# Moving work between engines in a two-branch kernel: damping buffers, attention first, transposing loads, reciprocals on ScalarE

One Trainium2 chip, one core. The metric is device time in microseconds (us); lower is better. A single core has no neighbour to compare it with, so "fast" and "slow" below only mean: within or over 1.5% of the fastest run of the same kernel in the same call.

## The reference, cut to what matters

Two branches over 2048 positions and 448 channels, side by side in the output.

```python
# A: linear attention, 16 heads of 28, features are softmax(+p) and softmax(-p)
q, k, v = split(x @ wqkv)
phi_k = concat(softmax(k @ w_phi), softmax(-(k @ w_phi)));  phi_q likewise
o = (phi_q @ (phi_k.T @ v)) / (phi_q @ sum(phi_k) + 1e-6)
a = o @ wo
# B: a long convolution by FFT; its kernel comes from 256 states per channel
K = einsum(C, exp(dt * A * l), dt * B).real        # l = 0..2047
y = irfft(rfft(u) * rfft(K)) + u * Dskip
return concat([a, y], -1)                           # bf16
```

## The kernel before

Every operation is recorded with its engine and issued in a fixed, searched order (a list of operation numbers); a second list gives the PSUM banks, a third the operations that go to an alternative engine. So an engine that waits is never overtaken by later work of its own. Branch B goes through the channels in four quarters: `rotations` (sines), `hi_tables`, `dampings` (exponentials), `tables` (products, VectorE), `scatter_k`, then spectra and convolution. The parts that the argument touches:

```python
xT = sb(oX, [112, 4, 2048])                      # x transposed: contraction in 4 chunks of 112 rows
Wp = [sb(o, [112, 4, 448]) for o in (155392, 158976)]   # query and key weights, w_phi folded in
WV = sb(162560, [112, 4, 448])

def recip(o, a):                                  # twelve of these: 8 key pairs, 4 query tiles
    prog.add("V", lambda: low(lambda: nc.vector.reciprocal(o, a)))

def key_side():
    for pr in range(8):                           # 8 pairs of 128-position tiles
        EK = sb(177920 + 3584 * (pr % 2), ...)    # two buffers
        ET = sb(209216, [128, 14, 128])           # one buffer
        for t in range(2):
            mms(acc(psum[:, b4, 0:448], [(xT[:, dj, ts_], Wp[1][:, dj, :]) for dj in range(4)]))
            mms(acc(psum[:, b5, 0:448], [(xT[:, dj, ts_], WV[:, dj, :]) for dj in range(4)]))
            ...                                   # exponentials to EK, values to V
        # EK -> ET by a transposing DMA on the SyncE queue
        ...                                       # ET @ HZ: sums per head, into PSUM
        recip(rk, psum[:, bz, 0:64])
        mul(VR, V, rk)                            # VectorE
        ...                                       # EK.T @ VR added up in PSUM
```

x and the query and key weights were transposed by TensorE (`flip_x`, `fold_weights`). [cut: tables, spectra, convolution]

The softmax here doesn't subtract the row's maximum and nothing guards it: scores larger than these inputs give would overflow.

## Time and profile before

| | before |
|---|---|
| median of 3 runs | 288.65 us (286.94 to 290.14) |
| span of the profiled run | 284.6 us |
| busy: PE, DVE, ACT | 236.7, 255.6, 202.2 us |
| table loads of ScalarE | 11 |
| matmul instructions | 3932 |

The prediction below shows the stages and groups. Three more views of the kernel before are needed later. First the page's chain of work that ended last (shares of the span by engine), and its row of the granted TensorE clock in 40 slices:

```profile
DVE 36%; PE 32%; DMA 15%; issue 7%; ACT 5%; SPq 3%; POOL 1%; DVEq 0%; POOLq 0%
```

```profile
PEclk9999999999999999999779999998999959999999
```

Then what weight loads (PEld) waited for (sum, times, longest), and the groups of matmuls with 448 and 512 columns (busy, mean ns):

```profile
PEld L203 <- issue: 28.3, 68, 1.9
```

### The profile page before, as it was taken

What the parts mean: (1) busy time and instruction counts of PE and PEld (TensorE: products, weight loads), DVE (VectorE), ACT (ScalarE), POOL (GpSimd) and SP (SyncE); (2) the same over time, 40 slices, a digit from 0 to 9 for tenths busy, and PEclk for the clock granted to TensorE, in tenths of its full rate; (3) what the DMA queues carried; (4) which work ended last, traced back from release to release, by engine and by line L of the source; (5) the groups of instructions that cost most, each with busy time, mean ns of one, the idle gap of its engine ahead of it and who ended that gap; (6) DMA issues with size and microseconds to landing.
All of it is one profiled execution on the core that took longest, in us unless ns stands there. A gap on an engine that the chain in (4) does not pass through costs nothing.

```text
span 284.6 us, 8940 instructions
## 1 busy us (share of the span) xinstructions
PE 236.7 (83%) x3932; PEld 179.9 (63%) x3932; DVE 255.6 (90%) x285; ACT 202.2 (71%) x340; POOL 16.1 (6%) x32
## 2 busy tenths in 40 slices
PE   1149899999999999999288977896989789897884
PEld 1149565756556587746187435782577789896874
DVE  4497999999999999799999999997999999499990
ACT  3759998989769989997899886869376224524241
POOL 8012101200000000000000010000000100000000
PEclk9999999999999999999779999998999959999999
DMA  7999375675353432513062648187789384747043
GB/s 166 229 232 243 89 209 120 142 191 129 67 131 65 67 131 59 83 36 87 6 137 46 134 118 323 19 191 222 281 267 324 72 275 85 192 59 155 2 99 68
DMA packets 64071, 39.49 MB, mean 139 GB/s; under 512 B 46736, under 2 KB 59424, under 8 KB 63648
## 3 DMA queue, kind: packets, MB, share of 16 engines
q1 hardware_dynamic: 61024, 31.57, 46.6%
q0 software_dynamic: 3008, 7.34, 8.2%
q8 instruction: 31, 0.51, 0.8%
q14 instruction: 8, 0.07, 0.1%
HBM read 26.36 MB, written 8.85 MB: 124 GB/s over the span
## 4 chain that ended last, share of the span: by engine, by line
DVE 36%; PE 32%; DMA 15%; issue 7%; ACT 5%; SPq 3%; POOL 1%; DVEq 0%; POOLq 0%
DVE sbuf L164 33%; PE psum L203 31%; DMA sbuf<-SCd 7%; DMA sbuf<-in_A_x_dram 5%; ACT sbuf L192 3%; SPq L218 3%; ACT sbuf L195 2%; DMA SCd<-sbuf 1%; DVE sbuf L189 1%; DVE sbuf L176 1%; DMA out_dram<-sbuf 1%; DMA sbuf<-in_B_u_dram 1%; PE psum L213 1%; POOL sbuf L218 1%; ACT L192 0%
## 5 line engine op out<-in xcount | busy, mean ns | idle before, releaser
L203 PE MATMUL psum<-sbuf 128*16 128x48 bf16 (+10 forms) x3824 | 229.0, 256 | 36.0 <-DVE sbuf L164 10.5
L203 PEld LDWEIGHTS <-sbuf 128*16 128x16 bf16 (+4 forms) x3824 | 171.5, 109 | 91.1 <-issue 28.3
L164 DVE TENSOR_TENSOR sbuf<-sbuf 128x896 bf16<-128x896 bf16 (+13 forms) x220 | 217.2, 1033 | 10.4 <-PE psum L203 3.5
L195 ACT CAST sbuf<-psum 128x448 bf16<-128x448 f32 (+4 forms) x128 | 70.9, 605 | 55.7 <-PE psum L203 54.1
L192 ACT ACTIVATE sbuf<-psum 128x448 bf16<-128x448 f32 (+4 forms) x140 | 83.9, 668 | 9.9 <-PE psum L203 9.7
L192 ACT ACTIVATE sbuf<-psum,sbuf 128x896 bf16<-128x896 f32 (+3 forms) x28 | 21.9, 814 | 4.4 <-DVE sbuf L164 2.3
L195 DVE CAST sbuf<-psum 128x896 bf16<-128x896 f32 (+2 forms) x13 | 12.4, 974 | 7.7 <-ACT sbuf L192 5.7
L213 PE MATMUL psum<-sbuf 128*112 128x128 bf16 (+2 forms) x108 | 10.3, 259 | 8.2 <-DVE sbuf L164 7.0
L213 PEld LDWEIGHTS <-sbuf 128*112 128x112 bf16 (+2 forms) x108 | 9.1, 165 | 9.8 <-DMA sbuf<-in_A_x_dram 5.5
L192 ACT ACTIVATE sbuf<-sbuf 128x896 bf16<-128x896 bf16 (+3 forms) x13 | 11.8, 905 | 4.6 <-DVE sbuf L164 3.9
L192 ACT ACT_TABLE_LOAD x11 | 14.1, 1283 | 0.9 <-PEq L909 0.7
L218 POOL DMA_DIRECT2D sbuf<-const x4 | 2.2, 551 | 118.3 <-PE psum L203 118.1
L218 POOL DMA_DIRECT2D sbuf<-in_B_u_dram x8 | 6.5, 827 | 18.1 <-PE psum L213 17.8
L176 DVE TENSOR_SCALAR sbuf<-sbuf 128x896 bf16<-128x896 bf16 (+3 forms) x8 | 4.9, 609 | 1.7 <-ACT sbuf L192 1.5
L182 ACT COPY sbuf<-psum 128x128 f32<-128x128 f32 (+2 forms) x10 | 4.3, 427 | 2.6 <-PE psum L213 2.1
L218 POOL DMA_DIRECT2D sbuf<-SUd x4 | 2.1, 528 | 69.3 <-DVE sbuf L164 42.3
L164 DVE TENSOR_TENSOR sbuf<-psum,sbuf 128x128 f32<-128x128 f32 (+3 forms) x10 | 4.7, 492 | 0.5 <-ACT sbuf L182 0.4
L176 ACT ACTIVATE sbuf<-sbuf 128x448 bf16<-128x448 bf16 (+1 forms) x3 | 4.4, 1455 | 0.9 <-DVE sbuf L164 0.9
L189 DVE RECIPROCAL sbuf<-psum 128x64 bf16<-128x64 f32 x8 | 4.4, 550 | 0.1
L182 DVE COPY sbuf<-psum 112x1024 bf16<-112x1024 bf16 x6 | 4.1, 684 | 0.3 <-PE psum L213 0.2
L179 DVE SCALAR_TENSOR_TENSOR sbuf<-sbuf 128x64 f32<-128x64 f32 (+1 forms) x6 | 3.0, 505 | 0.0
L198 POOL MEMSET sbuf<- 128x32 bf16 (+3 forms) x6 | 1.4, 258 | 18.4 <-DVE sbuf L164 18.1
(17 smaller groups left out, 18.4 us busy)
## 6 DMA issues: line engine op xcount, KB each, us to landing
sbuf<-const SPq DMA_DIRECT2D x16, 384.0 KB, 4.9
SUd<-sbuf SPq DMA_DIRECT2D x8, 448.0 KB, 3.7
sbuf<-SCd SPq DMA_DIRECT2D x16, 224.0 KB
sbuf<-SUd POOLq DMA_DIRECT2D x4, 896.0 KB, 5.6
sbuf<-const POOLq DMA_DIRECT2D x2, 1024.0 KB, 7.4
sbuf<-in_A_x_dram SPq DMA_DIRECT2D x4, 448.0 KB, 15.0
out_dram<-sbuf SPq DMA_DIRECT2D x4, 448.0 KB, 3.2
sbuf<-in_B_u_dram SPq DMA_DIRECT2D x16, 112.0 KB, 3.1
```

The source lines that it names most:

```text
L164: prog.add("V", lambda: nc.vector.tensor_tensor(out=o, in0=a, in1=b, op=op))
L176: prog.add("V", lambda: nc.vector.tensor_scalar_mul(o, a, s), lambda: nc.scalar.activation(o, a, ACT.Copy, scale=s))
L179: prog.add("V", lambda: nc.vector.scalar_tensor_tensor(out=o, in0=a, scalar=s, in1=b, op0=op0, op1=op1))
L182: prog.add("V", lambda: nc.vector.tensor_copy(o, a), lambda: nc.scalar.copy(o, a))
L189: prog.add("V", lambda: low(lambda: nc.vector.reciprocal(o, a)))
L192: prog.add("A", lambda: nc.scalar.activation(o, a, fn, **kw))
L195: prog.add("A", lambda: nc.scalar.copy(o, a), lambda: nc.vector.tensor_copy(o, a))
L198: prog.add("G", lambda: nc.gpsimd.memset(o, v))
L203: nc.tensor.matmul(o, lhsT=l, rhs=r, **kw)
L213: nc.tensor.transpose(o, i, idn)
L218: prog.add(eng, lambda: e.dma_start(out=o, in_=i))
```

## The change

The intent: give the damping factors of the last quarter a buffer of their own, finish attention before the convolution starts (so that ScalarE, idle late, takes copies there), make VectorE's convolution products fewer and larger, and take work off TensorE and VectorE: half of x, the query weights and u's rows are transposed by DMA, u times Dskip becomes a matmul, and seven of twelve reciprocals become exp(-ln) on ScalarE. The diff, cut to its core:

```diff
-    def recip(o, a):
-        prog.add("V", lambda: low(lambda: nc.vector.reciprocal(o, a)))
+    def recip(o, a, t):
+        def by_exp():
+            nc.scalar.activation(t, a, ACT.Ln)
+            nc.scalar.activation(o, t, ACT.Exp, scale=-1.0)
+        prog.kind[len(prog.ops)] = "L"
+        prog.add("V", lambda: low(lambda: nc.vector.reciprocal(o, a)), by_exp)
+    # run(order, warm): warm() ahead of each run of exponentials that holds such a reciprocal
+    warm = lambda: nc.scalar.activation(sb(138112, [128, 1], F32), bias_hp, ACT.Ln)

-    xT = sb(oX, [112, 4, 2048]);  Wp, WV = [112, 4, D_MODEL]
+    xT = sb(oX, [128, 4, 2048]);  Wp, WV = [128, 4, D_MODEL]
+    def chunk(t, dj, *at):                        # 448 = 128 + 128 + 128 + 64
+        v = t[64:128, 3] if dj == 3 else t[:, dj]
+        return v[(slice(None),) + at]
-    mms(acc(..., [(xT[:, dj, ts_], Wp[1][:, dj, :]) for dj in range(4)]))
+    mms(acc(..., [(chunk(xT, dj, ts_), chunk(Wp[1], dj)) for dj in range(4)]))   # V, Q likewise

+    def flip(o, i):
+        prog.add("S", lambda: nc.sync.dma_start(out=o, in_=i, transpose=True))
+    def load_x_flipped(t):                        # second half of x: eight of these
+        flip(xq[:, 0:3, t, 256:512], x2[1024 + t::4, 0:384])
+        flip(xq[:, 3, t, 256:512], x2[1024 + t::4, 320:448])
+    def load_folded(which):                       # query weights: four
+        flip(wT[:, which, c, :], A_wqkv[:, c0:c0 + 128])

-        return sb((oW, 174336, 174336, oW)[qt], [128, 31, QC])       # damping factors
+        return sb((oW, 174336, 174336, oPW)[qt], [128, 31, QC])
-    dampings(3); tables(3); conv_loads(1, *CT); conv(1, *CT, (6, 7))
+    dampings(3); scatter_k(2); conv_loads(1, *CT); conv(1, *CT, (6, 7)); tables(3)
     # [cut: query_side(0..3) all before tables(1); products over both spectra at once;
     #  u * Dskip as a matmul with a diagonal; new order, banks and alternative engines]
```

The 128-row chunks come with the transposing loads: they are written in blocks of 128 channels, so the last chunk holds channels 320 to 447, of which rows 64 to 127 are new.

## The prediction

> **What bounds the kernel now.** I read the page first, then the busy time of each engine by stage, then the groups kept apart by shape, then the timeline where a stage ends. The page's totals and its rows of 40 slices:
>
> ```profile
> PE 236.7 (83%) x3932; PEld 179.9 (63%) x3932; DVE 255.6 (90%) x285; ACT 202.2 (71%) x340; POOL 16.1 (6%) x32
> ...
> DVE  4497999999999999799999999997999999499990
> ACT  3759998989769989997899886869376224524241
> ```
>
> DVE is full from slice 3 to the end. ACT is nearly as full until slice 28 (200 us) and then half empty. So ACT's 71% is an average of two stages. I cut the span where DVE begins the damping products of each quarter of the model's channels (57.7, 121.3, 157.3, 198.1 us):
>
> ```profile
> core 0: us, PE busy (x) PEld busy (x) DVE busy (x) ACT busy (x) POOL busy (x), PEclk, DMA share, GB/s
> 0.00:57.70 57.70, 40.58 (x406) 29.66 (x407) 47.30 (x55) 45.29 (x62) 12.89 (x26) 1.00 0.78 181
> 57.70:121.30 63.60, 61.80 (x923) 41.41 (x922) 60.12 (x69) 56.07 (x93) 0.00 (x0) 1.00 0.44 98
> 121.30:157.30 36.00, 28.33 (x606) 20.87 (x605) 35.38 (x43) 32.68 (x57) 0.00 (x0) 0.91 0.30 68
> 157.30:198.10 40.80, 32.62 (x597) 22.34 (x596) 38.46 (x41) 32.56 (x51) 1.59 (x3) 0.98 0.60 168
> 198.10:284.60 86.50, 73.37 (x1410) 65.58 (x1408) 74.36 (x82) 35.63 (x82) 1.57 (x3) 0.95 0.58 156
> ```
>
> In the columns after the length: PE, PEld, DVE, ACT, POOL busy. Stages 1 to 4 are DVE's (and PE's in the second), with ACT at 80 to 91%. Stage 5 (convolution) belongs to DVE and PE together; ACT has 51 us to spare there. The groups by shape that I use (busy, mean ns):
>
> ```profile
> L164 DVE TENSOR_TENSOR sbuf<-sbuf 128x3584 bf16<-128x3584 bf16 x35 | 70.2, 2021 | 0.8 <-ACT sbuf L195 0.3
> L164 DVE TENSOR_TENSOR sbuf<-sbuf 128x896 bf16<-128x896 bf16 x66 | 38.9, 622 | 1.0
> L164 DVE TENSOR_TENSOR sbuf<-sbuf 128x1792 bf16<-128x1792 bf16 x36 | 38.3, 1090 | 4.0 <-PE psum L203 3.5
> L189 DVE RECIPROCAL sbuf<-psum 128x64 bf16<-128x64 f32 x8 | 4.4, 550 | 0.1
> ```
>
> ```profile
> L192 ACT ACT_TABLE_LOAD x11 | 14.1, 1283 | 0.9 <-PEq L909 0.7
> ```
>
> The place that the first part of the change aims at is the head of stage 5, in the timeline of ACT and then of DVE:
>
> ```profile
> 192.51 1.28 ACT L192 ACT_TABLE_LOAD   x1
> 193.81 6.59 ACT L192 ACTIVATE sbuf<-psum 128x224 bf16<-128x224 f32 x11
> ```
>
> ```profile
> 198.12 0.63 DVE L176 TENSOR_SCALAR sbuf<-sbuf 128x1792 bf16<-128x1792 bf16 x1 [1.54 <-ACT sbuf L192]
> ...
> 200.43 1.91 DVE L164 TENSOR_TENSOR sbuf<-sbuf 128x3360 bf16<-128x3360 bf16 x1 [0.39 <-ACT sbuf L192]
> ```
>
> The last damping factors are made late, since they lie in the buffer of the rotated tables; DVE waits for them twice, 1.9 us in all. That is all that this wait costs.
>
> **What the Trainium skill says.** (1) "ScalarE: Activation LUTs", What ACT_TABLE_LOAD costs: about 1283 ns, plus a drain of about 1380 ns. The trace agrees on the first, 1283 ns in 11 loads; the drain isn't seen as extra time (a copy ends at 192.50, the load starts at 192.51, the next activation at 193.81). (2) The same page, Table sets: natural logarithm and exponential share one set, so one after the other should need one load. The kernel before has no logarithm, so no trace here shows it; the built program of the changed kernel contradicts it, see below. (3) "DMA: Bandwidth & Descriptors", DMA Transpose (X-bar): transposes run in the DMA, from the SP or ACT queue, for two-byte types. The trace has eight, of 128 x 1792 elements, which land in 4.0 us after some 1.5 us of the SP queue; I take that size for the new ones.
>
> **The change, part by part**, from the built order of both kernels.
>
> *DVE.* The convolution's products become larger, fewer instructions: 9 of 3584 columns go (-18.2 us), 3 of 7168 come (+11.7, scaled from 3.65 us for 6720), 3 more of 2x1792 (+6.1), 8 more of 1792 in sum (+8.7; twelve come, and the four of u times Dskip go, which PE now does with a diagonal matrix), 24 of 896 go (-14.9). That is -6.6 us, nearly all in stage 5. Seven of twelve reciprocals move to ACT: -3.9. The rest comes to about nil. DVE: 255.6 to 245.
>
> *PE.* 112 matmuls fewer: half of x, the query weights and a second set of arguments for the angles go (about -12 us of 236.7). The 816 matmuls of 128x112 (43.7 us) in stage 5 stay.
>
> *ACT.* Each moved reciprocal is a logarithm and an exponential of 64 columns. The kernel puts a dummy logarithm ahead of such stretches, plainly so that a set holding both functions stays loaded. In the built program this fails: every logarithm loads a set without the exponential, and the next exponential loads the old set again. It has **26 table loads in place of 11**: +15 x 1.283 = +19.2 us. The small activations themselves are 16 x 0.25 = +4. Rates 3, 11 and 13 in place of a second group of four: +7. Query exponentials over two banks: 32 x 0.606 to 16 x 1.06 = -2.4. Wider or moved copies: -10. Sum about +17: ACT 202 to 219, and since stage 5 loses 7, stages 1 to 4 gain 23.
>
> Now by stage. I add every ACT and DVE instruction of the new order between the same marks at its mean duration from the groups, less 0.074 us each for ACT (my sum for before is 227.5 against 202.2 busy over 340: neighbours overlap).
>
> - Stage 1: ACT 55.6 (was 45.3, five loads more) and some 9 idle at the start as now: 63 (now 57.7).
> - Stage 2: ACT 66 (was 56.1, four moved reciprocals of two loads each), DVE 53; with 2 us for the chain exponential, transpose, sum, reciprocal, product, which now has 3.1 us of reciprocal where it had 0.55: 68 (now 63.6). ACT has taken DVE's place.
> - Stage 3: ACT 40.5 (five loads more than it needs), DVE 39: 42 (now 36.0).
> - Stage 4: DVE 33.5, ACT 28: 35 (now 40.8). The own buffer pays here: damping factors no longer wait for PE to have read the tables, and attention is done.
> - Stage 5: DVE 70 after its start (was 74.4), then the last two inverse transforms and the store, 7 us as now (277.2 to 284.6), and 2.5 of waits, of which there are 5 now: 79.5 (now 86.5).
>
> Sum 63 + 68 + 42 + 35 + 79.5 = 287.5 against 284.6. Untraced runs take 288.65 - 284.6 = 4.05 more than the span: **291.5 us**. In words: about 13 us are gained late, on DVE, and 16 are lost early, on ACT.
>
> **The rivals.** (A) *The loads hide.* ACT had 21.8 us idle between 20 and 200 us, so 19 could fit. Then DVE keeps the bound: 284.6 - 10.5 of DVE work - some 5 of waits = 269, or 273 us. For it: DVE's order is fixed and it hardly waited for ACT so far. Against it: stage 3 has ACT at 91% already, and ACT's order is fixed too, so a load stands in front of whatever comes next; a product waits behind its reciprocal. It would also go this way if the program that runs had fewer loads than the one built here. (B) *The loads cost in full.* If ACT also stalls for its inputs in stages 1 to 3 as it does now (some 15 us there), while it carries 23 more, stage 5 starts near 218 rather than 208, and the time is about 301. For it: one buffer for the transposed exponentials ties ACT's next pair to DVE's product. Against it: an engine that is late finds its inputs ready. (C) *The new transposes stall the SP queue*: sixteen more, at 1.5 us of queue and 4 us to landing. In the early stage DMA is at 0.78 already and stores of the signal's spectrum stand behind them. But x's second half is needed only by the fifth pair of key tiles, and u's rows only in stage 5, at 0.58; I give this 0 to 3 us. (D) *PE becomes stage 5's bound*: 43.7 us of inverse transforms and spectra all after the last tables. DVE has 48 us beside them, so about equal; a granted clock below 1 there (0.95 now) would cost 2 to 3 us.
>
> **Range and chances.** The centre lies between A (273) and B (301), nearer B, since the loads are counted and not guessed. 8 in 10: 279 to 301. Faster by over 2% means under 282.9, which needs A at least by half: 0.2. Slower by over 2% means over 294.4, a step of 3 us from the centre: 0.33. Within: 0.47.
>
> **What would show it.** Right: 26 table loads of 1.28 us; ACT busy 215 to 222 and DVE 243 to 248; ACT at 95% or more from 60 to 170 us, DVE with waits for ACT of several us in stages 2 and 3 where it has almost none now; the first product of the last quarter at 203 to 213 us; some 79 us from there to the end; no wait for damping factors there. Wrong: 11 to 14 loads; DVE above 95% from 60 to 200 us; the last quarter's products before 195 us; a wait for a transposed tile of over 3 us; PE waiting for rows of u; the tail of stage 5 longer than 84 us.

## More of the kernel before

```profile
L203 PE MATMUL psum<-sbuf 112*128 112x448 bf16 x256 | 54.6, 360 | 2.4 <-DVE sbuf L164 2.1 <-ACT sbuf L195 0.3
...
L203 PE MATMUL psum<-sbuf 112*112 112x512 bf16 x64 | 16.1, 381 | 0.8 <-ACT sbuf L195 0.7
```

Read "112*128 112x448": 112 rows of contraction, 128 columns of weights, 448 columns streamed. The chain is VectorE's first, TensorE's second; weight loads wait 28 us in all, in 68 places, for nothing that the profile names.

The kernel before scatters by up to 2.6% within a call (282.63 to 289.88 us).

## The result, and the profile after

The changed kernel is **slower**: 309.62 us median (308.96 to 311.04, four runs, all fast) against 287.79 (286.36 to 290.14). Ratios here are the mean time of one kernel's fast runs over that of the other's in the same rounds, so not quite the ratio of these medians: 1.0756, 95% interval 1.0668 to 1.0845. That is outside the predicted range.

The changed kernel's page: totals, rows of 40 slices, and the chain that ended last.

```profile
PE 244.9 (80%) x3820; PEld 167.7 (55%) x3820; DVE 248.4 (81%) x256; ACT 217.9 (71%) x350; POOL 16.3 (5%) x32
...
PEclk9999799977989997997999667796998999999999
...
PE 42%; DVE 23%; DMA 13%; ACT 10%; issue 8%; SPq 3%; DVEq 0%; ACTq 0%
```

TensorE has 112 matmuls fewer and is busy 8 us **longer**. The chain has gone from VectorE to TensorE, and the clock row has many more slices of 6 to 8 than before. Busy time by stage, cut at the same marks as in the prediction (columns: length, PE, PEld, DVE, ACT, POOL, clock, DMA share, GB/s):

```profile
0.00:72.94 72.94, 48.09 (x398) 25.90 (x398) 51.93 (x61) 53.52 (x84) 13.02 (x26) 0.93 1.04 156
72.94:145.68 72.74, 64.44 (x887) 38.02 (x887) 55.83 (x63) 59.80 (x97) 0.00 (x0) 0.93 0.31 75
145.68:191.48 45.80, 37.97 (x626) 23.25 (x625) 38.20 (x43) 42.60 (x69) 1.12 (x2) 0.85 0.41 118
191.48:228.12 36.64, 28.28 (x488) 17.86 (x488) 35.22 (x32) 28.65 (x48) 0.53 (x1) 0.86 0.63 146
228.12:306.80 78.68, 66.17 (x1424) 62.64 (x1423) 67.18 (x61) 33.38 (x56) 1.58 (x3) 0.98 0.63 155
```

| stage | before | predicted | after |
|---|---|---|---|
| 1 | 57.7 | 63 | 72.9 |
| 2 | 63.6 | 68 | 72.7 |
| 3 | 36.0 | 42 | 45.8 |
| 4 | 40.8 | 35 | 36.6 |
| 5 | 86.5 | 79.5 | 78.7 |

The late stages are as predicted: 12 us won. Stages 1 to 3 miss by 10, 5 and 4 us. What VectorE waited for longest in the changed kernel (L204 is the exponential of a moved reciprocal, L206 a reciprocal left on VectorE, L222 a matmul):

```profile
DVE sbuf L177 <- ACT sbuf L204: 10.6, 4, 4.0
DVE sbuf L206 <- PE psum L222: 7.2, 2, 4.3
```

Its groups of table loads, 26 in all, by the line that needed them:

```profile
L211 ACT ACT_TABLE_LOAD x10 | 12.8, 1283 | 0.9 <-PEq L998 0.7
...
L203 ACT ACT_TABLE_LOAD x7 | 9.0, 1283 | 0.1
L204 ACT ACT_TABLE_LOAD x7 | 9.0, 1283 | 0.1
```

Its weight loads and matmuls with 64 rows, and the wait of weight loads for nothing that is named ("issue"):

```profile
L222 PEld LDWEIGHTS <-sbuf 64*128 64x128 bf16 x32 | 3.0, 94 | 14.1 <-issue 14.1
L222 PEld LDWEIGHTS <-sbuf 64*112 64x112 bf16 x16 | 2.0, 128 | 6.6 <-issue 6.6
```

```profile
L222 PE MATMUL psum<-sbuf 128*128 128x448 bf16 x224 | 54.3, 381 | 5.1 <-ACT sbuf L214 2.6 <-DMA sbuf<-const 1.1 <-DVE sbuf L214 0.8
...
L222 PE MATMUL psum<-sbuf 64*112 64x512 bf16 x16 | 7.2, 451 | 0.0
```

```profile
PEld L222 <- issue: 77.4, 184, 2.7
```

The timeline of weight loads, in one stretch of the key side, shows where these gaps lie:

```profile
78.65 0.30 PEld L222 LDWEIGHTS <-sbuf 128*128 128x128 bf16 x3 [0.20 <-issue]
79.32 0.09 PEld L222 LDWEIGHTS <-sbuf 64*128 64x128 bf16 x1 [0.37 <-issue]
79.62 1.54 PEld L222 LDWEIGHTS <-sbuf 112*128 112x128 bf16 x27 [0.20 <-issue]
81.53 0.09 PEld L222 LDWEIGHTS <-sbuf 64*128 64x128 bf16 x1 [0.37 <-issue]
```

Within these runs of 128- or 112-row loads no gap is listed. There is one of 0.37 us before each 64-row load and one of 0.20 us after it: with 48 such loads an estimate of 0.57 x 48 = 27 us over the kernel. The Trainium skill, "TensorEngine Tiling (Array Packing)", Key Properties, has a sentence that may fit: "Changing tiling mode (not just tile) drains the TensorE". No run here shows that 64 rows count as another mode; what the traces show is that a change between 112 and 128 rows, with 112 or 128 columns of weights and nothing named to wait for, leaves mostly 0 to 0.09 us, and that each of the 48 changes to 64 rows leaves the gap.

A third suspect stands in the chain of the changed kernel, in order of time (start, us, what):

```profile
55.59 12.26 DMA sbuf<-sbuf
67.85 0.05 issue
67.89 12.15 PE psum L222 x85
```

The third transpose of key features took 12.3 us to land; the prediction's size was 4.0, which the profile gives for one transpose of eight. TensorE waited for it, and the clock fell around it:

```profile
60.00:70.00 10.00, 5.69 (x47) 2.40 (x46) 5.38 (x6) 7.24 (x16) 0.00 (x0) 0.78 1.23 120
70.00:80.00 10.00, 10.00 (x71) 4.35 (x71) 6.96 (x14) 4.79 (x7) 0.00 (x0) 0.88 0.48 90
```

The skill's "TensorE: Matmul & The Clock Gate", Part 1, says that an idle window of about 3.4 us throttles the array; TensorE's longest wait in 20 to 75 us was 4.3 us, and in the kernel before the clock was 1.00 up to 121 us. That fits, but a long wait is not all that lowers the clock here. In the changed kernel it also fell where TensorE was busy throughout and had waited 2.1 us at most since 86 us:

```profile
116.80:120.20 3.40, 3.40 (x16) 1.63 (x15) 3.40 (x7) 2.36 (x3) 0.00 (x0) 0.50 0.02 5
```

What brings that about is not shown. The mean granted clock was 0.92 in the changed kernel against 0.97 in the kernel before, and no run separates that from the causes below.

So three theories, which do not exclude each other. **T1**: the reciprocals on ScalarE and their 15 extra table loads. **T2**: the transposing loads of x and query weights. **T3**: the 64-row chunk. T1 and T2 were in the prediction as rivals B and C. T3 was in no part of it.

### The profile page after: what moved, and what is told of

Its sections match the earlier page's. It is cut to its first block, busy times and chain, and to the rows that moved or that the text cites. A ratio compares the mean times of both kernels' runs of the same rounds, so it can differ in the third digit from the quotient of the medians.

```text
span 306.8 us, 8682 instructions
## 1 busy us (share of the span) xinstructions
PE 244.9 (80%) x3820; PEld 167.7 (55%) x3820; DVE 248.4 (81%) x256; ACT 217.9 (71%) x350; POOL 16.3 (5%) x32
## 4 chain that ended last, share of the span: by engine, by line
PE 42%; DVE 23%; DMA 13%; ACT 10%; issue 8%; SPq 3%; DVEq 0%; ACTq 0%
PE psum L222 42%; DVE sbuf L177 22%; DMA sbuf<-const 5%; DMA sbuf<-sbuf 4%; DMA sbuf<-in_B_B_re_dram 4%; ACT sbuf L211 3%; ACT sbuf L214 3%; ACT L203 2%; SPq L236 2%; SPq L240 1%; ACT sbuf L189 1%; ACT L204 0%; ACT sbuf L204 0%; PE psum L232 0%; ACT sbuf L203 0%
## 5 line engine op out<-in xcount | busy, mean ns | idle before, releaser
L222 PE MATMUL psum<-sbuf 128*16 128x48 bf16 (+9 forms) x3760 | 240.5, 260 | 52.7 <-DVE sbuf L177 11.6
L177 DVE TENSOR_TENSOR sbuf<-sbuf 128x1792 bf16<-128x1792 bf16 (+15 forms) x203 | 213.3, 1091 | 34.6 <-ACT sbuf L204 10.6
L222 PEld LDWEIGHTS <-sbuf 128*16 128x16 bf16 (+3 forms) x3760 | 163.5, 110 | 128.1 <-issue 77.4
L214 ACT CAST sbuf<-psum 128x448 bf16<-128x448 f32 (+3 forms) x93 | 66.0, 754 | 56.2 <-PE psum L222 51.7
L211 ACT ACTIVATE sbuf<-psum,sbuf 128x224 bf16<-128x224 f32 (+3 forms) x36 | 22.7, 701 | 0.0
L211 ACT ACT_TABLE_LOAD x10 | 12.8, 1283 | 0.9 <-PEq L998 0.7
L232 PE MATMUL psum<-sbuf 128*128 128x128 bf16 (+1 forms) x60 | 5.9, 245 | 5.4 <-DVE sbuf L177 3.4
L203 ACT ACT_TABLE_LOAD x7 | 9.0, 1283 | 0.1
L204 ACT ACT_TABLE_LOAD x7 | 9.0, 1283 | 0.1
L232 PEld LDWEIGHTS <-sbuf 128*128 128x128 bf16 (+1 forms) x60 | 4.7, 125 | 7.0 <-DVE sbuf L177 3.6
L206 DVE RECIPROCAL sbuf<-psum 128x64 bf16<-128x64 f32 x3 | 1.7, 555 | 7.2 <-PE psum L222 7.2
L189 DVE TENSOR_SCALAR sbuf<-sbuf 128x3584 bf16<-128x3584 bf16 (+3 forms) x7 | 5.0, 707 | 0.1
L189 ACT ACTIVATE sbuf<-sbuf 112x448 bf16<-112x448 bf16 (+3 forms) x4 | 3.8, 944 | 0.1
L177 DVE TENSOR_TENSOR sbuf<-psum,sbuf 128x896 bf16<-128x896 f32 (+2 forms) x6 | 3.5, 625 | 0.0
```

Source lines behind the costliest of these rows:

```text
L177: prog.add("V", lambda: nc.vector.tensor_tensor(out=o, in0=a, in1=b, op=op))
L189: prog.add("V", lambda: nc.vector.tensor_scalar_mul(o, a, s), lambda: nc.scalar.activation(o, a, ACT.Copy, scale=s))
L203: nc.scalar.activation(t, a, ACT.Ln)
L204: nc.scalar.activation(o, t, ACT.Exp, scale=-1.0)
L211: prog.add("A", lambda: nc.scalar.activation(o, a, fn, **kw))
L214: prog.add("A", lambda: nc.scalar.copy(o, a), lambda: nc.vector.tensor_copy(o, a))
```

## The experiments

Fourteen kernels. Medians are of all runs; "before" is the kernel before in the same call.

| label | median | before | fast ratio to before (95%) |
|---|---|---|---|
| (the changed kernel) | 309.62 | 287.79 | 1.0756 (1.0668 to 1.0845) |
| e1_one_set | 299.95 | 287.26 | 1.0607 (1.0473 to 1.0741) |
| e2_recip_dve | 300.89 | 287.26 | too few fast runs |
| e3_plain_x (wrong) | 299.38 | 287.26 | 1.0554 (1.0389 to 1.0718) |
| e4_rows128 | 296.72 | 287.26 | 1.0505 (1.0424 to 1.0585) |
| e5_set_rows | 285.70 | 287.27 | too few fast runs |
| e6_set_rows_plain (wrong) | 283.71 | 287.27 | 0.9937 (0.9834 to 1.0040) |
| e7_set_rows_pe (wrong) | 288.94 | 287.27 | 1.0048 (0.9935 to 1.0162) |
| e8_pairs (one run) | 305.70 | 287.27 | none |
| e9_order | 287.86 | 288.58 | 0.9992 (0.9926 to 1.0058) |
| e10_dve_rows | 286.89 | 288.58 | 0.9929 (0.9868 to 0.9990) |
| e11_pe_again | 294.85 | 288.58 | 1.0139 (1.0070 to 1.0209) |
| e12_two_moved | 304.98 | 284.73 | 1.0634 (1.0503 to 1.0765) |
| e13_wo_early | 303.70 | 287.41 | 1.0610 (1.0514 to 1.0706) |
| e14_repaired_wo_early | 285.53 | 287.41 | too few fast runs |

In the call of e1 to e4 only three of eight runs of the kernel before counted as fast (282.6 to 284.9), so its ratios lie higher than its medians say. Below, "won" is the drop of the median's distance from the kernel before, against the changed kernel's 21.8 us. It mixes fast and slow runs. By the fast ratios alone the wins are smaller: e1 4.3, e3 5.8, e4 7.2, e12 3.5, e13 4.2 us. So each size below is rough, to some 3 to 5 us.

### e1 and e2: the table loads

```diff
-    lambda: nc.scalar.activation(sb(138112, [128, 1], F32), bias_hp, ACT.Ln)       # e1
+    lambda: nc.scalar.preload_act_table_set("natural_log_exp_and_others")
-    (other if i in OTHER else fn)()                                                # e2
+    (other if i in OTHER and self.kind.get(i) != "L" else fn)()      # and no warm()
```

> The dummy logarithm ahead of each run of exponentials is replaced by an explicit load of the one table set that holds both functions; the built program then has 10 table loads in place of 26, so 16 x 1.283 us = 20.5 us less of ScalarE work. Theory T1 (the loads stand on the path: VectorE waited 10.6 us for ScalarE's exponential in the reciprocal and 7.2 us for PE behind it): 297 to 302 us, and those waits fall below 4 us. Rivals T2 (transposing loads of x hold up the early stages) and T3 (64-row contraction chunk slows TensorE): 306 to 310 us, because ScalarE is busy only 71% of the span and most loads fall into its gaps.

> All twelve reciprocals go back to VectorE, no logarithms at all; 10 table loads. T1: 296 to 302 us, at or a little below the one-set version, since a VectorE reciprocal took about 0.55 us against 3.1 us from logarithm to exponential. T2, T3: 306 to 310 us. If it is slower than the one-set version, the author's reciprocals on ScalarE are right once the loads are gone.

Both built to 10 table loads and both won 8 to 9 us (21.8 to 12.7, and to 13.6). In the one-set kernel VectorE's wait for the exponential is nearly gone:

```profile
DVE sbuf L177 <- ACT sbuf L204: 0.6, 1, 0.6
```

T1 holds, for some 9 of the 22 us. Its other sign failed: the wait for TensorE behind the reciprocal (L206) did not fall below 4 us, it was 10.1, so that wait was not the loads' (e13 below takes it to 1.1). Sixteen loads, 20.5 us of ScalarE, were worth 9 us of time, nearly all in stage 2 (72.7 to 64.6 us). The second finding is that reciprocals by ScalarE with the right set and by VectorE differ by less than the scatter.

### e3: the transposing loads

```diff
-    prog.add("S", lambda: nc.sync.dma_start(out=o, in_=i, transpose=True))     # x, query weights
+    prog.add("S", lambda: nc.sync.dma_start(out=o, in_=plain_rows_of_the_same_size))
```

> Wrong result on purpose: the twelve transposing loads of half of x and of the query weights become plain loads of about the same bytes into the same places at the same points of the order; the transposing loads of u and of the key features stay. T2: the first two stages shorten by 8 to 13 us together, total 297 to 302 us, the key-feature transposes land in about 4 us as before and the DMA share in 20 to 70 us falls below 1. T1, T3: 307 to 310 us.

It won 9.7 us. Taken alone that confirms T2. The DMA share in 20 to 30 us fell from 1.59 at 89 GB/s to 0.81 at 185 GB/s, so the plain loads do load the DMA engines far less (the share adds up packet times, so it can pass 1). The skill's "Advanced Engine Details and Errata", X-Bar Transpose (TRN2), says that transposing DMAs are as fast as regular ones; the profile gives the landing of one of the eight of x, 11.7 us (6.9 in e13, 14.7 in e2), and of one of the plain loads in their place, 6.4 (6.9 in e6), queueing included. So the trace speaks against it, on few landings. And the clock did not fall:

```profile
60.00:70.00 10.00, 9.83 (x75) 4.43 (x74) 9.05 (x15) 8.32 (x19) 0.00 (x0) 1.00 0.59 140
70.00:80.00 10.00, 9.65 (x88) 4.82 (x86) 8.91 (x4) 8.43 (x12) 0.00 (x0) 1.00 0.52 119
```

### e4 and e8: the 64-row chunk

```diff
-    v = t[64:128, 3] if dj == 3 else t[:, dj]                    # e4
+    v = t[:, dj]            # rows 0:64 of Wp[0][:, 3], Wp[1][:, 3], WV[:, 3] are set to zero
-    ... for dj in range(4)])])                                   # e8, query side only
+    ... for dj in (range(4), range(3, -1, -1))[k]])])
```

> The last contraction chunk of x and the weights is taken over all 128 rows, with rows 0 to 63 of the three weight blocks set to zero (two more small ScalarE copies, three POOL memsets), so the result stays right and each matmul has the same columns. T3 (a change between 64-row and 128-row tiles empties the array: weight loads of 64 rows idle 14.1 us and 6.6 us, PE 42% of the chain against 32%): PE idle of 15 to 20 us goes, of which 5 to 9 us on the path: 300 to 305 us; the mean of the 448-column matmuls falls from 390 to about 355 ns. T1, T2: 308 to 311 us.

> The changed kernel with the chunk order of every second query product turned round, so that the two 64-row matmuls of a pair stand side by side: as many 64-row matmuls, half as many changes between 64 and 128 rows on the query side. If the change of rows is what costs, the 6.6 us of idle before the sixteen 64-row weight loads of the query side fall to 3 to 4 us and the 64x512 matmul's mean falls from 451 ns; if a 64-row matmul is slow by itself, both stay. The time changes by less than 3 us either way: 306 to 310 us.

e4 does strictly more arithmetic than the changed kernel, and won 12.3 us, more than expected. PE is busy 232.6 us instead of 244.9, and the weight loads' unnamed wait fell by 19 us, as expected (15 to 20):

```profile
PEld L222 <- issue: 58.0, 103, 4.7
```

```profile
L222 PE MATMUL psum<-sbuf 128*128 128x448 bf16 x256 | 55.7, 369 | 5.2 <-ACT sbuf L214 2.8 <-ACT sbuf L203 1.3 <-DVE sbuf L214 0.7
```

The 32 matmuls with 64 rows and 448 columns had cost 12.7 us; as 32 more with 128 rows they add 1.4 to that group. The mean of that group fell from 381 to 369 ns only, not to the 355 expected. Two other things changed with the rows, so that the 12.3 us are not all theirs: the granted clock of the profiled run rose from 0.92 to 0.95, and TensorE's wait of 4.3 us for the key transpose is gone (see e13, which makes that worth up to 5.5 us). e8 says what it is about the 64 rows. It has as many 64-row matmuls, but on the query side two stand side by side, so TensorE goes over to 64 rows half as often there:

```profile
L222 PEld LDWEIGHTS <-sbuf 64*128 64x128 bf16 x32 | 3.0, 94 | 14.0 <-issue 14.0
L222 PEld LDWEIGHTS <-sbuf 64*112 64x112 bf16 x16 | 1.5, 132 | 3.5 <-issue 3.5
```

```profile
121.67 0.17 PEld L222 LDWEIGHTS <-sbuf 64*112 64x112 bf16 x2 [0.39 <-issue]
```

The query side's wait halved (6.6 to 3.5), the key side's, left as it was, stayed at 14; before the second load of a pair there is no gap, and the mean of the 64x512 matmul fell from 451 to 430 ns. So the gaps come with the going over, not with the 64 rows: T3 holds for its cause, while its size in time lies between some 7 and 12 us by medians. The time of e8 is one run, 3.4 us won, and the sum of all unnamed waits hardly moved (76.9 us), as other groups waited more; it only says that the sign is right.

### e5, e6, e10: together

e5 joins e1 and e4, e6 joins e1, e3 and e4, e10 joins e2 and e4.

> One table set for the reciprocals and the 128-row chunk together. Alone they took 9.7 and 12.9 us off 309.6. If the two costs are separate waits that stand on the path one after the other (T1 and T3 both true, independent): 286 to 289 us. If they cover each other (the same waits of VectorE seen twice): 293 to 297 us.

> As e5_set_rows, and with the transposing loads of half of x and of the query weights as plain loads (wrong result on purpose). Three independent costs: 309.6 - 9.7 - 12.9 - 10.2 = 276.8, so 275 to 280 us, faster than the kernel before, with the first three stages near the lengths predicted (63, 68, 42). If they overlap: 283 to 290 us.

> As e5_set_rows, with the reciprocals all on VectorE instead of on ScalarE with one table set. In the changed kernel the two repairs were worth the same (299.95 and 300.9 us), so 284 to 288 us here. If VectorE has become the engine that sets stage 2 (55.3 us busy of 56.1 in e5_set_rows), the added 3 us of it show in full: 287 to 289 us.

e5 won 23.4 us, against 9.1 + 12.3 = 21.4 for the sum of its parts: T1 and T3 (with the meeting that e4 removed unasked) are separate costs, and with both mended the changed kernel is level with the kernel before. Three of e5's four runs count as slow (285.3 to 290.3 beside one of 280.6), so no ratio stands, but all four are 19 us or more below the changed kernel's median. e10 confirms it with fast runs: 0.9929. What e3 had won alone did **not** add up: e6 was expected at 275 to 280, and won 2 us more than e5. So either T2 was not a cost of its own, or it was one that the other repairs removed as well.

### e7, e11, e9: other places for the same work

```diff
-    flip(...)                                                    # e7, e11, on top of e5
+    load_x(2); load_x(3); load of the query weights              # plain
+    nc.tensor.transpose(...) x 48, six copies out of PSUM
```

> Right result: as e5_set_rows, but the second half of x and the query weights are loaded plainly and transposed by TensorE as before the change, 48 small transposes and six copies out of PSUM (four of ScalarE, two of VectorE, about 1.1 us each). If the transposing loads were the cost, and not the bytes: 278 to 283 us, that is faster than the kernel before by 2 to 3%. If PE and ScalarE have no room for this in the first two stages: 285 to 290 us.

> What e7_set_rows_pe was meant to be, with the buffer that it shared with the reciprocals' temporaries and the banks that it shared with the key sums mended: second half of x and query weights transposed by TensorE, right result. e7's first stage took 73.9 us against 65.1. If its wrong banks made that: 63 to 66 us and a total of 283 to 286. If the 48 transposes and six copies have no room in stage 1: 70 us or more, 287 to 291 us, and the DMA transposes of the change were worth their place.

> As e5_set_rows (285.7 us median), with five operations moved in the order and nothing else: the two small products with Dskip, for which VectorE waited 3.1 us, go to where VectorE had a gap; the load of the cosine table goes ahead of the first two transposing loads; two transposing loads of x go behind the first key-feature transpose. If the transposing loads' cost was their place in the one queue that issues them: stage 1 shortens from 65 to 60 to 63 us, total 281 to 284 us. If it was their traffic: 284 to 287 us.

e7 gave a wrong result (relative error 0.14): its weight buffer overlapped the reciprocals' temporaries, and its transposes wrote into the banks in which the key sums are added up. e11 mends both and is right, and slower than e5 by 7.8 us (measured from the kernel before of each call): stage 1 takes 74.1 us, the second of the outcomes foretold. But its trace holds another cost, the meeting of two transfers that the next section finds: a key transpose took 10.65 us and TensorE waited 4.5 us for it. So how much of the 7.8 us is due to the 48 transposes and six copies is open, and that the change was right to take them off TensorE is not shown. e9 moved five operations to where the trace of e5 showed room, and won nothing (-0.7 us against the kernel before, e5 -1.6); its first stage became longer, 69.6 us. Room in one trace of a static order need not be room once something moves.

### e12, e13, e14: what was the 10 us of e3?

e12 moves two of the transposing loads of x away from the late key transpose. e13 moves one other load, that of the output weights `wo`, one place up on GpSimd; e14 does the same in e5. All are changes of the order alone.

```diff
-    ... 85 ... 118 151 ... 254 154 ...                           # e12: 151, 154 behind 85
+    ... 85 151 154 ... 118 ... 254 ...
-    ... 166 ... 162 ...        (162: dma("G", wo, A_wo))         # e13, e14
+    ... 162 166 ...
```

> The changed kernel with two of its eight transposing loads of x issued some 13 us earlier, into a gap of the queue at 44 to 48 us, in place of right behind the key-feature transpose that was issued at 55.6 us and took 12.3 us to land; same loads, same bytes, all else in its place. If the 10 us that the plain loads won in e3_plain_x were this one collision and the clock that fell after it: that transpose lands in 4 to 7 us, stage 1 shortens from 72.9 to 66 to 69 us, and the time is 300 to 305 us. If they were the traffic as such: 308 to 311 us, with another transfer late in its place.

> The changed kernel with the load of the output weights (392 KB) issued one place earlier on GpSimd, ahead of a memset for which GpSimd waited until 55.1 us, so near 43 to 50 us; everything else in place, all transposing loads kept. If the meeting of this load with the third key-feature transpose is what the plain loads of e3_plain_x avoided: that transpose lands in under 8 us instead of 12.3, stage 1 shortens from 72.9 to 66 to 69 us, the granted clock at 60 to 80 us rises from 0.78 and 0.88 to above 0.95, and the time is 300 to 305 us. If the transposing loads themselves slow it: 308 to 311 us, and the transpose still takes 10 us or more.

> The same move in the kernel of e5_set_rows (one table set, 128-row chunk; 285.7 us), where the load and the transpose did not meet. By the same theory nothing to win: within 2 us of e5, 284 to 288 us. If moving the load early helps by itself: 280 to 283 us.

e12 missed: the key transpose still took 11 us with nothing of x behind it, and only 1.6 us were won (3.5 by fast runs; its profile is of a slow run). That ruled out the loads that I had blamed for this transpose, and the traces together named another. The `wo` load in the changed kernel started 0.10 us after the late transpose:

```profile
55.69 0.76 POOL L240 DMA_DIRECT2D sbuf<-in_A_wo_dram  x1 [0.27 <-ACT sbuf L211]
```

In the changed kernel, e1, e2, e8, e11 and e12 it started 0.07 to 0.11 us after it and took 10.2 to 12.4 us itself; in e3, e4, e5, e6, e9 and e10 it started 0.6 to 0.9 us after it and took 5.8 to 7.7. The transpose took 10.7 to 12.7 us in the first group and 6.2 to 8.1 in the second, where it stands on the chain of work. e11 says most: it has no transposing load of x or of weights at all, and still

```profile
56.96 10.65 DMA sbuf<-sbuf
```

```profile
57.03 0.75 POOL L240 DMA_DIRECT2D sbuf<-in_A_wo_dram  x1 [0.28 <-ACT sbuf L211]
```

In e13 it starts at 44.6 us:

```profile
44.62 0.75 POOL L240 DMA_DIRECT2D sbuf<-in_A_wo_dram  x1
```

With all transposing loads in place, TensorE then waits for no transposed tile at all (4.3 us before), VectorE's wait behind it falls from 7.2 to 1.1 us, and the kernel won 5.5 us:

```profile
DVE sbuf L206 <- PE psum L222: 1.1, 1, 1.1
```

The landing of the key transpose itself is not on record in e13; its tile was used 9.5 us after the issue. By time alone e13 is not told from e12 (4.2 and 3.5 us by fast runs); it is the waits that tell them apart. The control e14 won 0.3 more than e5. So about half of what e3 seemed to show of the transposing loads was one meeting of two transfers. The kernel before has both, and there they don't meet (`wo` starts 1.3 us ahead of a transpose and takes 4.6 us). In these runs a shift of 0.5 to 0.8 us took them apart. e4 and e5 took it apart by chance, which would explain why the gains did not add up. Two details went otherwise than I wrote: stage 1 hardly shortened (72.4 us), the gain appeared in stage 2 (68.2), and the clock recovered in 70 to 80 us only (0.83, then 1.00). Why 0.1 us and 0.8 us of distance differ so much is not shown, and e3's other 4 us are not divided further.

The stages of e14, a fast run, are those of the change without its three faults:

```profile
0.00:65.02 65.02, 45.78 (x423) 30.13 (x424) 51.95 (x61) 50.47 (x84) 14.13 (x29) 0.97 1.13 173
65.02:121.75 56.73, 53.52 (x863) 36.59 (x862) 55.24 (x63) 48.93 (x89) 0.00 (x0) 1.00 0.41 98
121.75:165.41 43.66, 35.19 (x628) 23.56 (x627) 37.81 (x43) 40.38 (x69) 1.11 (x2) 0.85 0.50 135
165.41:202.40 36.99, 27.62 (x488) 17.79 (x487) 35.20 (x32) 24.64 (x42) 0.53 (x1) 0.85 0.54 135
202.40:281.10 78.70, 66.34 (x1424) 62.48 (x1423) 67.23 (x61) 33.35 (x56) 1.58 (x3) 0.98 0.59 153
```

Against the kernel before it loses 7 and 8 us in stages 1 and 3 and wins 7, 4 and 8 in stages 2, 4 and 5: VectorE sets stage 2 again (55.2 of 56.7). Why stages 1 and 3 stay longer is open; the plain loads of e6 leave stage 1 at 64.1 us. No version here beats the kernel before by more than its scatter; the best right ones, e10, e5 and e14, are about level with the kernel before.

## Why the prediction was wrong, point by point

- **Stages 4 and 5 were right**: 35 and 79.5 predicted, 36.6 and 78.7 measured, and within 3 us of that in every variant whose stages I cut, but e11, where the mark of stage 3 was lost. So was the reason: the own buffer and DVE's larger products.
- **Work on DVE and ACT was right in size**: DVE 245 and ACT 219 predicted, 248.4 and 217.9 measured; 26 table loads, as counted.
- **The step that failed is PE**: "112 matmuls fewer ... (about -12 us of 236.7)". PE got 8.2 us busier. I priced the matmuls by count and saw the new chunk widths only as shapes. Forty-eight of them have 64 rows between neighbours of 112 or 128, with 0.57 us of gaps each. e4 takes that away and wins 12 us, of which up to 5.5 can be the meeting; so 7 to 12 of the miss of 18 us (309.6 against 291.5). Without the three faults the count was not far off: PE is busy 228.4 us in e14.
- **"ACT has taken DVE's place" in stages 2 and 3 failed with it.** The sign I named, ACT at 95% or more from 60 to 170 us, is absent: it was busy 90.5 of 110 us, 82%, and PE 93.5. The chain is 42% PE. The loads did cost, but as latency in front of VectorE's product (10.6 us of waits), as the prediction also foretold, and not as the sum of ACT's work. I charged the reciprocals 2 us of latency in stage 2; taking their loads or the reciprocals themselves away won 8 to 9 us (e1, e2), most of it there, where the prediction had 16 lost early on ACT. Nor do the loads explain stages 1 and 3: e14, without them, still takes 65.0 and 43.7 us there (63 and 42 predicted with them), so those two numbers were near for a reason that I did not give.
- **Rival C was under-sized**: 0 to 3 us for the new transposes. e3 puts them at 9.7 in the changed kernel, of which e13 gives 5.5 to a meeting with another load; with the other faults mended 2 us are left (e6 against e5), as predicted. The prediction's own sign for it, a wait for a transposed tile of over 3 us, came true (4.3), but by luck: the tile was one of the key features, whose transposes the kernel before had too, and it met a load, not a full SP queue. The prediction also counted sixteen new transposes where the trace has twenty (8 of x, 4 of weights, 8 of u), and its 4.0 us is the landing of one transpose.
- **Rival B gave the nearest time** (301), by a mechanism that explains under half of it.
- **The range was too narrow** because it was spanned by one question, whether table loads hide. Two causes outside of that question added up.
- **A small term was misread**: 4.05 us from span to untraced time was a median less the span of another run. The profiled run of the kernel before took 286.73 us for its span of 284.6, that of the changed kernel 309.2 for 306.8, so 2.1 to 2.4.

Summed by medians: 9 us for table loads and logarithms, 12 for row changes with the meeting of two transfers, together 23 (e5): all of the difference between the kernels of 21.8. The meeting is inside these sums, since e4 and e5 removed it unasked; its share of e4's 12 is not separated, nor is that of the clock.

## What to carry to other kernels

When a tile's contraction is cut anew, look at the sequence of row counts on TensorE and not only at the number of matmuls: zero-padding a 64-row remainder to 128 rows cost 1.4 us of matmul time, the changes cost several times that. When two ScalarE functions are meant to share a table, count the loads in the built program, and load the shared set by name. And when single repairs win more than they do together, look for a coincidence in time that each of them happens to break; then move the one transfer, and run a control in which there was no meeting.

## What the Trainium skill lacked or had wrong

- "ScalarE: Activation LUTs", Table sets, promises one load for a logarithm followed by an exponential. The changed kernel had two for each of its seven moved reciprocals, 26 loads of 1283 ns in all; with the set that holds both loaded by name it had 10. The page doesn't say that the loads placed for a program can choose a set that holds one function only.
- "TensorEngine Tiling (Array Packing)", Key Properties, says that changing the mode drains TensorE, without a size, and speaks of tiles used side by side. Here a plain matmul with 64 rows among 112- and 128-row ones had gaps of 0.37 us before and 0.20 us after its weight load, and two with 64 rows side by side had none between them; that this is the page's change of mode is not shown.
- "Advanced Engine Details and Errata", X-Bar Transpose (TRN2), calls transposing DMAs as fast as regular ones. Here one of x landed in 11.7 us, a plain one in its place in 6.4 (one landing in each run, queueing included), with the DMA share at 1.59 against 0.81 in the same 10 us.
- No page has it: a GpSimd-issued load of 392 KB that started 0.07 to 0.11 us after a transposing DMA between buffers took 10.2 to 12.4 us in six kernels, and 5.8 to 7.7 us in six where it started 0.6 to 0.9 us after it; where the transpose stands on the chain of work, it took 10.7 to 12.7 us in the first case and 6.2 to 8.1 in the second.
